# Transposes moved behind the first key block's product, a stack loaded in one piece, and four sums and three stores given to other engines

## The chip, the cores and the metric

The kernel runs on one core of a Trainium2 chip. A core has five engines with a queue of instructions each: TensorE (PE; its weight loads are shown apart as PEld), VectorE (DVE), ScalarE (ACT), GpSimd (POOL) and SyncE (SP), which here does nothing but issue DMA transfers. An engine takes its instructions in order and waits on semaphores for the others. The metric is the device time of one execution in microseconds (us); lower is better.

## The reference, cut to what matters

A block of a transformer on 2048 tokens of width 576: a modulated layer norm, attention with 32 heads of width 18 in four segments of 512 tokens with a memory carried from segment to segment, an output projection with a residual, a second modulated layer norm and a gated feed-forward network of width 4608 with a residual. All in float32.

```python
for s in range(N):                                   # N = 4 segments, L = 512
    qs, ks, vs = q[:, :, s], k[:, :, s], v[:, :, s]
    logits = jnp.einsum("bhqd,bhkd->bhqk", qs, ks) * scale + mask
    p = _softmax(logits, axis=-1)
    a_dot = jnp.einsum("bhqk,bhkd->bhqd", p, vs)
    pq = phi(qs)
    num = jnp.einsum("bhld,bhde->bhle", pq, M)
    den = jnp.einsum("bhld,bhd->bhl", pq, z)[..., None] + 1e-6
    o = g * (num / den) + (1.0 - g) * a_dot
    outs.append(o)
    pk = phi(ks)
    M = M + jnp.einsum("bhld,bhle->bhde", pk, vs)
    z = z + jnp.einsum("bhld->bhd", pk)
...
x = x + ga * (o @ wo)
h = _layernorm(x, axis=-1) * (1 + cb) + sb
x = x + gb * ((_silu(h @ w_gate) * (h @ w_up)) @ w_down)
```

## The kernel before

The program has four stages, one after the other on TensorE.

**Projections (0 to 245 us).** Queries, keys and values of all segments; queries and keys go to DRAM, split in a high and a low part so that products can run in the fast float32 format.

**Attention units (245 to 610 us).** The attention is cut into 32 units u, each of four heads of one segment (s = u // 8, q = u % 8). Four buffers hold the operands of a unit: `ks` (keys) and `qs` (queries), called a stack here; unit u uses buffer u % 4. `load_stack` (L159) fills one with four DMAs, two for each half e of its rows. In a unit two streams run side by side, written out by hand: `p2_step` (L584) forms the scores of unit u transposed (L601), their exponentials on ScalarE (L604) and a triangular cut on GpSimd (L608); `p1_step` (L173) forms the scores of unit u + 2 (L182) and their row maxima on VectorE (L187, two score banks in turn), which `mt_a` and `mt_b` transpose and `put_m` stores into two rows of that unit's stack.

A unit has 11 steps k. Each step issues a piece of both streams and then the events of the table `PAT` (L60), which has four patterns: 0 and 1 for even and odd units of the first half of a segment, 2 and 3 for even and odd units of the second half. An event is a letter; those that matter here:

- `V0` to `V3`: the products of exponentials and values for the four key blocks (`av_step`, L621). V0 and V1 belong to unit u, V2 and V3 to unit u - 1, whose sum is copied out by `E` (`ev_step`).
- `c`: four transposes of that copied output of unit u - 1 on TensorE (`comb_a`, L642) into a bank of the tag `x`, of which there are two.
- `d`: its division by the softmax sums (`comb_b`, L650 to L658 on VectorE, L659 on GpSimd).
- `M0` to `M3` and `X`: a piece of the output projection of the segment before (`wo_m`, L731) and its residual add (`wo_x`, L736), which also stores the row tile; `R`, `S`, `T`: the transposes of its input (`wo_r`, L704) and their split.
- `m`, `n`: transposing and storing the maxima of unit u + 1; `A`, `B`, `C`, `D`, `G`: the memory term.

What orders the loads is the place of their calls in this loop (L1352, L1366), since SyncE takes them in turn:

```python
load_unit(u + 3, 0)
...
for k in range(11):
    ...
    if k == 5:
        load_unit(u + 3, 1)
```

**The last output projection (610 to 636 us).** The projection of segment 3 runs by itself: eight groups of 14 matmuls (L731), four row tiles i times two halves h, in two banks in turn, so that a group needs the residual add (L736) of the group two before. Beside it VectorE and ScalarE prepare the first operands of the next stage: `y_here` (L1046 to L1050), `prep_r` (L1153, L1154), `prep_w` (L1168, L1169). `sum_o` (L1156) forms sums of the weight tiles `O`; the list `SS` names the eight places n = 8i + 4h + c of the loop where one is called. ScalarE issues the stores of the first three row tiles, SyncE that of the fourth.

**The feed-forward network (636 to 1899 us).** Products by a fast scheme with seven multiplications (L1204), then the down projection (L1308, L1325).

Of the kernel before, what the change touches and what calls it, by code (L numbers as in the profile page):

```python
# [15 lines left out]
P = 128  # L16
S = 2048
D = 576
# [39 lines left out]
E1 = 3  # L58
E2 = 2
PAT = (["", "V2", "V3 E m D", "M0", "n M1 Q G", "c", "M2 d", "V0 g", "h A0 q M3 R S X", "T Y Z B0", "A1 P V1 z B1 f C"],  # L60
# [3 lines left out]
LNA = 1  # L64
S1B, S2B, XB, WB = 2, 2, 2, 1

# [1 line left out]
def f32(ap):  # L68
    return ap.bitcast(F32)
# [3 lines left out]
def block(ctx: ExitStack, tc: tile.TileContext, x, wqk, wv, wo, beta, wgu, wd, c, w_mod, out):  # L73
    nc = tc.nc
    def pool(stk, name, bufs=1, **kw):
        return stk.enter_context(tc.tile_pool(name=name, bufs=bufs, reuse_waits="tile", **kw))
# [5 lines left out]
    def chain(*g):  # L82
        for a in g:
            yield from a

    def run(g):
        for _ in g:
            pass
# [26 lines left out]
    NB = 4  # L115
# [29 lines left out]
    xD = [dr.tile([P, 4, D], F32, tag=f"xD{s}", name=f"xD{s}") for s in range(NSEG)]  # L145
# [9 lines left out]
    NU = len(units)  # L155
    mcol, pmt, mrow = {}, {}, {}

    def load_stack(u, b, es=(0, 1)):
        s, q = units[u]  # L159
        for e in es:  # L160
            v = [d[s].rearrange("f z t -> (f z) t").rearrange("(Q a e r) t -> Q e r a t", Q=8, a=2, e=2)[q, e]
                 for d in (kD, qD)]
            r = slice(54 * e, 54 * e + 54)
            nc.sync.dma_start(f32(kst[b][r]), v[0])
            nc.sync.dma_start(f32(qst[b][r, e:4:2, :]), v[1])
# [79 lines left out]
    with ExitStack() as p1:  # L245
# [78 lines left out]
        with ExitStack() as p0:  # L324
# [41 lines left out]
            for b in range(3):  # L366
                n = P if b < 2 else 64
# [89 lines left out]
        def proj(s, t):  # L457
            hh, hl, hr = hT[s]
            pp = ps.tile([P, L], F32, tag="p", name="pp", bufs=3)
            mm14(pp, lambda k: wqkh[:, t, k, :], lambda k: wqkl[:, t, k, :], lambda k: hh[k],  # L460
                 lambda k: hl[k], lambda: hr, True)
            f = pb.tile([P, L], F32, tag="pf", name="pf")
            fh = pb.tile([P, L], F32R, tag="fh", name="fh")
            fl = pb.tile([P, L], F32R, tag="fl", name="fl")
            nc.scalar.copy(fh, pp)
            nc.scalar.copy(f, pp)
            nc.vector.tensor_tensor(fl, f, f32(fh), op=ALU.subtract)
            k0, k1 = 128 * t, min(128 * t + 128, D)
            if k0 < D:
                n = k1 - k0  # L470
                nc.sync.dma_start(kD[s][k0:k1, 0:2, :], f32(fh[:n]).unsqueeze(1).to_broadcast([n, 2, L]))
                nc.sync.dma_start(kD[s][k0:k1, 2, :], f32(fl[:n]))
            q0, q1 = max(128 * t - D, 0), 128 * t + 128 - D
            if q1 > 0:
                n = q1 - q0
                r = P - n
                nc.sync.dma_start(qD[s][q0:q1, 0:3:2, :], f32(fh[r:]).unsqueeze(1).to_broadcast([n, 2, L]))
                nc.sync.dma_start(qD[s][q0:q1, 1, :], f32(fl[r:]))
                if s > 0:
                    nc.sync.dma_start(qF[s][q0:q1, :], f[r:])  # L480
            return f
# [34 lines left out]
        for s in range(NSEG):  # L516
# [5 lines left out]
            g = chain(*gens)  # L522
# [6 lines left out]
            for t in QKORD:  # L529
# [4 lines left out]
                f = proj(s, t)  # L534
# [41 lines left out]
    opl_ = pool(p2, "op2")  # L576
    ps = pool(p2, "ps2", 2, space=PSUM)

    def load_unit(u, e):
        if u < NU:  # L580
            load_stack(u, u % NB, (e,))

    def p1_seq(u):
        if NE <= u < NU:  # L584
            for i in range(4):
                yield from p1_step(u, u % NB, 3 - i, ps, wk, 4)
# [3 lines left out]
    def p2_step(u, j):  # L590
        if u >= NU:
            return
        n = L - 128 * j
        per = L // n if n <= 256 else 1
        pt = pp_.tile([P, 4, n], F32, tag=f"P{j}", name="Pt", bufs=1)
        Pt[u, j] = pt
        for h in range(0, 4, per):
            bank = ps.tile([P, L], F32, tag="s2", name="s2", bufs=S2B)
            for g in range(h, h + per, 2):
                w = min(per, 2)  # L600
                nc.tensor.matmul(bank[:, n * (g - h):n * (g - h + w)].rearrange("p (a b) -> p a b", a=w),  # L601
                                 lhsT=kst[u % NB][0:110, g // 2, 128 * j:128 * j + 128],
                                 rhs=qst[u % NB][0:110, g:g + w, 128 * j:L], start=True, stop=True)
            nc.scalar.activation(pt[:, h:h + per, :n], bank[:, :n * per].rearrange("p (a b) -> p a b", a=per),  # L604
                                 AF.Exp, scale=SCALE)
            if h + per < 4:
                yield
        nc.gpsimd.affine_select(out=pt[:, :, :P], in_=pt[:, :, :P], pattern=[[0, 4], [1, P]], compare_op=ALU.is_ge,  # L608
                                fill=0.0, base=0, channel_multiplier=-1)
        yield  # L610
# [52 lines left out]
    def load_v(s, j):  # L663
        if j == 0:
            vq[s] = vp.tile([P, 4, VC], F32, tag="vq", name=f"vq{s}")
        nc.sync.dma_start(vq[s][:, j, :], vD[s][:, j, :])
# [5 lines left out]
    op = pool(p2r, "op", side="right")  # L672
# [37 lines left out]
    def wo_s(s, i):  # L710
        nc.scalar.copy(oT[s, i][0], pto[s, i])
# [21 lines left out]
    def wo_x(s, i, h):  # L733
        xr = oT[s, i][2]
        sl = slice(288 * h, 288 * h + 288)
        nc.vector.tensor_tensor(xr[:, sl], wps[0][:, :288], xr[:, sl], op=ALU.add)  # L736
        if h == 1 and s < 3:
            (nc.scalar if (s, i) == (2, 3) else nc.sync).dma_start(xD[s][:, i, :], xr)

    lnv = {}  # L740
# [386 lines left out]
    O, W, R, RW, DP = {}, {}, {}, {}, {}  # L1127
    later = []

    def flush():  # L1130
        while later:
            later.pop(0)()
# [20 lines left out]
        nc.scalar.copy(r[0:96, c], o[0:96, c, 2, :])  # L1153
        later.append(lambda: nc.vector.tensor_tensor(r[32:64, c], o[32:64, c, 2, :], f32(r[32:64, c]), op=ALU.subtract))  # L1154

    def sum_o(p, z, j):  # L1156
        o = O[p, z]
        d, a, b, op = ((4, 3, 2, ALU.add), (5, 4, 0, ALU.subtract), (3, 0, 3, ALU.subtract), (6, 1, 5, ALU.subtract))[j]
        nc.gpsimd.tensor_tensor(o[:, d], o[:, a], o[:, b], op=op)  # L1159

    def store_r(p, z):
        nc.scalar.dma_start(rD[p][z], f32(R[z][0:96]))
# [44 lines left out]
    T, SG, AC, AP = {}, {}, {}, {}  # L1207
# [136 lines left out]
    with tc.manual_schedule():  # L1344
# [4 lines left out]
        event("f", -1)  # L1349
        for u in range(NU + 1):  # L1350
            s, q = divmod(u, 8)
            load_unit(u + 3, 0)  # L1352
            ga = chain(*[p2_step(u, j) for j in range(4)])
            gb = p1_seq(u + 2)
            for k in range(11):
                next(ga, None)
                next(gb, None)
                if u == 17 and k == 0:
                    stage_a()
                if u == 24 and k == 0:  # L1360
                    stage_b()
                for ev in PAT[q // 4 * 2 + u % 2][k].split():
                    event(ev, u)
                for f in sched.pop(11 * u + k, ()):
                    f()
                if k == 5:  # L1366
                    load_unit(u + 3, 1)
                    if 3 <= q < 7 and s < 3:
                        load_v(s + 1, q - 3)
            run(ga)  # L1370
            run(gb)
        p2.close()
# [9 lines left out]
        xr3 = {i: load_xr(3, i) for i in range(3)}  # L1382
# [20 lines left out]
        for i in range(4):  # L1403
            for h in range(2):
                for c in range(WC):
                    n = 8 * i + 4 * h + c
                    wo_m(3, i, h, c, 2)
                    if c == 3:
                        wo_x(3, i, h)
                    flush()  # L1410
                    if i > 0 and h == 0 and c == 1:
                        nc.scalar.dma_start(xD[3][:, i - 1, :], xr3[i - 1])
                    if n in SS:
                        j = SS.index(n)
                        sum_o(0, j // 4, j % 4)
                    if n in HH:
                        y_here(HH.index(n))
                    if n in WW:
                        j = WW.index(n)
                        if j < 2:  # L1420
                            prep_r(0, 0, 0, j)
                        prep_w(0, 0, next(gw))
                if h == 1 and i < 2:
                    wo_r(3, i + 2)
                    wo_s(3, i + 2)
                    wo_t(3, i + 2)
        flush()
        nc.sync.dma_start(xD[3][:, 3, :], xr3[3])
        p2r.close()
        p5.close()  # L1430
        accp = pool(p4, "acc")
# [10 lines left out]
        n, nw = 0, PF  # L1442
# [5 lines left out]
        for t in range(2):  # L1448
            for p in range(NPR):
# [16 lines left out]
                for k in range(14):  # L1466
                    z, m = ZM[k]
# [67 lines left out]
                    if prev is not None and is_plain(*prev):  # L1535
# [3 lines left out]
                        if CH0[t][k]:  # L1539
                            f = plain(*prev, chunk)  # L1540
# [20 lines left out]
                    if is_plain(t, p):  # L1561
                        if k in DK[dl // 2]:
                            j = DK[dl // 2].index(k)
# [74 lines left out]
```

## Time and profile before

| | |
|---|---|
| time, median of 3 runs | 1902.11 us (1901.88 to 1902.49) |
| the profiled execution | 1901.1 us, of which the span from the first to the last instruction is 1899.4 us |
| granted TensorE clock, mean | 0.998 |
| busy in the span | PE 98%, PEld 82%, DVE 79%, ACT 51%, POOL 28% |
| largest groups on the chain that ended last | PE A L1204 24%, PE pd L1325 13%, PE C L1204 12%, PE pd L1308 9% |

How to read the profile's rows. A row of the timeline gives the start in us from the span's beginning, the length, engine, line of the kernel, operation, output and inputs by the program's names, the shape and a count of merged instructions; in brackets stands the idle time of the engine before it and what ended that. Matmuls are pipelined, so the distance from one start to the next is what one costs, and its length is longer. A row of the windows gives, for each engine, its busy time in that stretch. A row of the list of waits gives who waited for whom, the total, how often, and the longest.

### The profile page before, as it was taken

The numbers are of one execution on the slowest core, as the hardware profiler recorded it, in microseconds if no ns is written. First come the engines' busy times: TensorE is split into PE (matmuls) and PEld (weight loads), VectorE is DVE, ScalarE is ACT, GpSimd is POOL, SyncE is SP. The second block draws the span as 40 slices with busy tenths as digits, with TensorE's granted clock in tenths as the row PEclk, the third lists the DMA queues.
The fourth block names the chain that finished last, engine by engine and source line by source line (L and its number), as shares of the span: only waits on it lengthen the run. The fifth ranks groups of instructions, "written<-read, shape, count | busy, mean of one in ns | idle before, by whom it ended". The sixth has DMA issues, their size and how long they took to land.

```text
span 1899.4 us, 30695 instructions
## 1 busy us (share of the span) xinstructions
PE 1866.3 (98%) x10927; PEld 1559.4 (82%) x10927; DVE 1497.0 (79%) x3275; ACT 972.1 (51%) x2128; POOL 535.8 (28%) x717
## 2 busy tenths in 40 slices
PE   7999999999999899999999999999999999999999
PEld 5888856676766788888888888888888888888888
DVE  6555368878886888888888888867888888888887
ACT  4433377768766544454454454444445454454542
POOL 2000046454556544454445445400000000000000
PEclk9999999999999999999999999999999999999999
DMA  7767654546654854554554544477233332333331
GB/s 248 258 202 256 227 156 132 138 132 181 184 158 150 301 175 165 176 168 156 171 174 150 191 149 143 152 259 234 93 124 102 106 104 93 124 102 107 104 103 61
DMA packets 179424, 304.31 MB, mean 160 GB/s; under 512 B 26152, under 2 KB 107688, under 8 KB 177352
## 3 DMA queue, kind: packets, MB, share of 16 engines
q1 hardware_dynamic: 150264, 244.40, 41.4%
q10 hardware_dynamic: 29008, 57.96, 8.6%
q8 instruction: 86, 1.41, 0.3%
q14 instruction: 66, 0.54, 0.1%
HBM read 187.98 MB, written 113.77 MB: 159 GB/s over the span
## 4 chain that ended last, share of the span: by engine, by line
PE 91%; DVE 4%; DMA 2%; ACT 1%; issue 1%; SPq 1%; POOL 0%; ACTq 0%; DVEq 0%
PE A L1204 24%; PE pd L1325 13%; PE C L1204 12%; PE pd L1308 9%; PE B L1204 6%; PE pp L99 6%; PE s L601 4%; PE av L621 4%; PE s L182 3%; PE pv L99 3%; PE pw L731 2%; DMA qs<-qD 2%; PE pm L449 1%; PE pn L802 1%; DVE junk L187 1%
## 5 line engine op out<-in xcount | busy, mean ns | idle before, releaser
L1204 PE MATMUL A<-y,wh 128*128 128x512 f32 x1152 | 405.9, 393 | 1.0 <-ACT cu L1233 0.7
L187 DVE CUSTOM_DVE_ANT_0 junk<-s,tri 128x256 bf16<-128x256 f32 (+3 forms) x512 | 229.2, 487 | 74.4 <-PE s L182 67.1
L1169 DVE TENSOR_TENSOR wl<-O,wh 128x256 fp32r<-128x256 f32 x504 | 260.3, 521 | 2.8 <-ACT wh L1168 2.3
L1204 PEld LDWEIGHTS A<-y,wh 128*128 128x128 f32 x1152 | 216.6, 188 | 44.6 <-ACT cu L1233 1.1
L604 ACT ACTIVATE Pt<-s 128x512 f32<-128x512 f32 (+1 forms) x352 | 187.9, 559 | 76.2 <-PE s L601 69.7
L1204 PE MATMUL A<-y,wl 128*128 128x512 f32 x576 | 226.7, 394 | 0.0
L1159 POOL TENSOR_TENSOR O<-O 128x384 f32<-128x384 f32 x144 | 162.9, 1145 | 165.7 <-DMA O<-in_wgu_dram 71.3
L1313 DVE TENSOR_TENSOR acc<-acc,pd 128x576 f32<-128x576 f32 x216 | 162.3, 752 | 58.7 <-PE pd L1308 51.9
L1204 PE MATMUL C<-y,wh 128*128 128x512 f32 x576 | 202.6, 392 | 2.6 <-DVE cu L1227 2.6
L1168 ACT CAST wh<-O 128x256 fp32r<-128x256 f32 x504 | 196.8, 405 | 7.4 <-DVE wl L1169 3.5
L1325 PE MATMUL pd<-dh,ah 128*128 128x288 f32 x640 | 189.0, 295 | 0.0
L1325 PE MATMUL pd<-dh,al 128*128 128x288 f32 x640 | 189.0, 295 | 0.0
L1325 PE MATMUL pd<-dl,ah 128*128 128x288 f32 x640 | 188.8, 295 | 0.0
L1329 DVE TENSOR_TENSOR acc<-acc,pd 128x576 f32<-128x576 f32 x156 | 116.9, 749 | 88.8 <-PE pd L1325 88.5
L1268 ACT CAST ah<-sg 128x512 fp32r<-128x512 f32 x192 | 119.1, 620 | 82.0 <-DVE sg L1228 81.7
L601 PE MATMUL s<-qs,ks 110*128 110x512 f32 (+2 forms) x384 | 150.1, 407 | 2.1 <-ACT Pt L604 2.0
L182 PE MATMUL s<-ks,qs 108*128 108x256 f32 (+3 forms) x512 | 140.9, 327 | 6.0 <-DMA qs<-qD 3.5
L1269 DVE TENSOR_TENSOR al<-sg,ah 128x512 fp32r<-128x512 f32 x192 | 133.5, 695 | 9.1 <-ACT ah L1268 8.9
L1308 PE MATMUL pd<-dh,ah 128*128 128x288 f32 x448 | 133.0, 297 | 0.0
L1308 PE MATMUL pd<-dh,al 128*128 128x288 f32 x448 | 132.5, 296 | 0.0
L1308 PE MATMUL pd<-dl,ah 128*128 128x288 f32 x448 | 132.3, 295 | 0.0
L1204 PEld LDWEIGHTS C<-y,wh 128*128 128x128 f32 x576 | 108.3, 188 | 23.2 <-DVE cu L1227 3.0
(360 smaller groups left out, 4392.4 us busy)
## 6 DMA issues: line engine op xcount, KB each, us to landing
O<-in_wgu_dram SPq DMA_DIRECT2D x36, 768.0 KB
oD<-O ACTq DMA_DIRECT2D x36, 512.0 KB
O<-oD SPq DMA_DIRECT2D x36, 512.0 KB
ks<-kD SPq DMA_DIRECT2D x64, 216.0 KB
qs<-qD SPq DMA_DIRECT2D x64, 216.0 KB
O<-in_wgu_dram SPq DMA_DIRECT2D x36, 384.0 KB
rD<-wr ACTq DMA_DIRECT2D x36, 336.0 KB
wr<-rD SPq DMA_DIRECT2D x35, 336.0 KB
```

The lines of the kernel that those rows point to most:

```text
L99: nc.tensor.matmul(ps, lhsT=a, rhs=b, start=(k == 0), stop=(k == 13))
L182: nc.tensor.matmul(bank[:, n * (h - h0):n * (h - h0) + n], lhsT=qst[b][0:108, h, 128 * i:128 * i + 128], rhs=kst[b][0:108, h // 2, 0:n], s ...
L187: nc.vector.tensor_tensor_reduce(junk[:, :n], bank[:, n * (h - h0):n * (h - h0) + n], tri[:, L - n:], 1.0, -3e38, op0=ALU.add, op1=ALU.max ...
L601: nc.tensor.matmul(bank[:, n * (g - h):n * (g - h + w)].rearrange("p (a b) -> p a b", a=w), lhsT=kst[u % NB][0:110, g // 2, 128 * j:128 * ...
L604: nc.scalar.activation(pt[:, h:h + per, :n], bank[:, :n * per].rearrange("p (a b) -> p a b", a=per), AF.Exp, scale=SCALE)
L1159: nc.gpsimd.tensor_tensor(o[:, d], o[:, a], o[:, b], op=op)
L1168: nc.scalar.copy(wh, o)
L1169: later.append(lambda: nc.vector.tensor_tensor(wl, o, f32(wh), op=ALU.subtract))
L1204: nc.tensor.matmul(bank, lhsT=a, rhs=b, start=(first and n == 0), stop=(n == 6), skip_group_check=not first)
L1308: nc.tensor.matmul(pd[:, i, :288], lhsT=a[:, tk], rhs=w, start=(k == 0), stop=(k == 2))
L1313: nc.vector.tensor_tensor(o, o, pd[:, :, :288], op=ALU.add)
L1325: nc.tensor.matmul(pd[:, i, :288], lhsT=a[:, tk], rhs=w, start=(k == 0), stop=(k == 5))
```

## The change

```diff
-       ["V2 D", "l M0 Q", "V3 m E", "M1", "G p n A0 B0 M2", "", "M3 X A1 q c x d B1", "f", "V0 g", "", "C V1 Y h P"],
-       ["", "V2", "V3 m E", "M0", "D G M1 c n", "", "Q V0 d g R", "h", "M2 q M3 A0 S B0 X", "Z Y", "P f z V1 A1 T B1 C"],
-       ["", "V2 m", "l D n p G M0", "V3", "M1 E M2 A0", "", "M3 x c", "B0", "V0 d Q", "A1 g", "q X V1 Y B1 h P C f"])
+       ["V2 D", "l M0 Q", "V3 m E", "M1", "G p n A0 B0 M2", "", "M3 X A1 q x B1", "f", "V0 c g", "d", "C V1 Y h P"],
+       ["", "V2", "V3 m E", "M0", "D G M1 n", "", "Q V0 c R d g", "h", "M2 q M3 A0 S B0 X", "Z Y", "P f z V1 A1 T B1 C"],
+       ["", "V2 m", "l D n p G M0", "V3", "M1 E M2 A0", "", "M3 x", "B0", "V0 c Q d", "A1 g", "q X V1 Y B1 h P C f"])
...
-    def load_unit(u, e):
+    def load_unit(u):
         if u < NU:
-            load_stack(u, u % NB, (e,))
+            load_stack(u, u % NB)
...
-        if h == 1 and s < 3:
+        if h == 1:
             (nc.scalar if (s, i) == (2, 3) else nc.sync).dma_start(xD[s][:, i, :], xr)
...
-    def sum_o(p, z, j):
+    def sum_o(p, z, j, eng=nc.gpsimd):
...
-        nc.gpsimd.tensor_tensor(o[:, d], o[:, a], o[:, b], op=op)
+        eng.tensor_tensor(o[:, d], o[:, a], o[:, b], op=op)
...
-            load_unit(u + 3, 0)
+            load_unit(u + 3)
...
-                if k == 5:
-                    load_unit(u + 3, 1)
-                    if 3 <= q < 7 and s < 3:
-                        load_v(s + 1, q - 3)
+                if k == 5 and 3 <= q < 7 and s < 3:
+                    load_v(s + 1, q - 3)
...
-                    if i > 0 and h == 0 and c == 1:
-                        nc.scalar.dma_start(xD[3][:, i - 1, :], xr3[i - 1])
                     if n in SS:
                         j = SS.index(n)
-                        sum_o(0, j // 4, j % 4)
+                        sum_o(0, j // 4, j % 4, nc.vector if j > 3 else nc.gpsimd)
...
-        nc.sync.dma_start(xD[3][:, 3, :], xr3[3])
```

In patterns 1, 2 and 3 the event `c` now stands directly behind `V0`: from step 6 to step 8 in pattern 1, from 4 to 6 in pattern 2, from 6 to 8 in pattern 3. The event `d` moves from step 6 to step 9 in pattern 1; in patterns 2 and 3 it keeps its step, which is now that of `c`. Pattern 0 is as it was. All four DMAs of a stack are issued at step 0 of the unit. In the last output projection the last four of the eight sums run on VectorE, and SyncE issues all four stores, each directly behind the residual add of its row tile. Nothing that is computed changes.

More of the change, by code (lines that the diff above doesn't have):

```diff
@@ L156, in block, with load_stack @@
     mcol, pmt, mrow = {}, {}, {}
-    def load_stack(u, b, es=(0, 1)):
+    def load_stack(u, b):
         s, q = units[u]
-        for e in es:
+        for e in range(2):
             v = [d[s].rearrange("f z t -> (f z) t").rearrange("(Q a e r) t -> Q e r a t", Q=8, a=2, e=2)[q, e]
```

## The prediction

> **What bounds the kernel now.** I read the windows first, one row per stage; columns are the stretch and its length, busy us of TensorE, its weight loads, VectorE, ScalarE and GpSimd, granted clock, DMA share, GB/s.
>
> ```profile
> core 0: us, PE busy (x) PEld busy (x) DVE busy (x) ACT busy (x) POOL busy (x), PEclk, DMA share, GB/s
> 245.00:610.00 365.00, 356.21 (x2597) 238.48 (x2596) 289.03 (x1176) 270.91 (x557) 201.16 (x382) 1.00 0.53 149
> 610.00:636.00 26.00, 21.91 (x152) 21.05 (x151) 18.93 (x31) 9.54 (x21) 14.74 (x12) 0.93 0.85 317
> 636.00:1310.00 674.00, 670.25 (x3663) 588.32 (x3662) 560.54 (x860) 319.47 (x740) 294.51 (x265) 1.00 0.55 182
> ```
>
> TensorE (PE) is the bound in every stage. The diff touches two: the attention units (245 to 610 us) and the last output projection (610 to 636 us), which has 4.1 us of open idle and a clock of 0.93. What follows holds PE 670.25 of 674 us, so time won before it should arrive at the end nearly whole. Then the list of waits of the attention stage (total us, times, longest):
>
> ```profile
> PEld s L182 <- DVE mx L187: 10.3, 22, 1.3
> PE s L182 <- DMA qs<-qD: 3.5, 6, 0.9
> ```
>
> PE's waits there are short and few, for VectorE's running maxima and for the stack's query half.
>
> **The change part by part.**
>
> **Transposes behind the product.** 24 units (patterns 1, 2 and 3, eight each) issue the same four transposes (L642) later; only the neighbours change. Here is the transposes' cost alone, the product of key block 0 (L621, 512 wide) alone, and the product with other transposes (L704) directly behind it, which pattern 2 already has.
>
> ```profile
> 391.55 1.07 PE L621 MATMUL av<-Pt,vq 128*32 128x512 f32 x8
> ...
> 392.89 0.28 PE L182 MATMUL s<-ks,qs 108*128 108x256 f32 x1
> ...
> 399.75 0.60 PE L642 MATMUL px<-ident,avs 128*128 128x128 f32 x4
> ...
> 400.36 0.34 PE L182 MATMUL s<-ks,qs 108*128 108x384 f32 x1
> 400.54 0.34 PE L601 MATMUL s<-qs,ks 110*128 110x384 f32 x1
> ...
> 400.98 1.07 PE L621 MATMUL av<-Pt,vq 128*32 128x512 f32 x8
> 401.98 0.66 PE L704 MATMUL pto<-ident,o 128*128 128x128 f32 x4
> ...
> 402.65 0.34 PE L182 MATMUL s<-ks,qs 108*128 108x384 f32 x1
> ```
>
> From start to start, less the one score matmul in between (0.18 for 384 columns, 400.36 to 400.54; 0.24 for 512, in the next fence): product alone 1.34 - 0.24 = 1.10, transposes alone 0.61 - 0.18 = 0.43, both together 1.67 - 0.18 = 1.49. Together they cost 0.04 to 0.06 less than 1.53. Units 19, 25 and 27 and six of pattern 2 have transposes behind that product already, so 15 of 24 gain: 15 x 0.05 = 0.8 us. Bounds: 0.6 (15 x 0.04) to 1.2 (24 x 0.05).
>
> **The stack at step 0.** SyncE issues the second half's two DMAs (ks, qs) right behind the first half's, not behind the two stores of step 4. The number of DMAs is the same.
>
> ```profile
> 429.92 0.29 SPq L164 DMA_DIRECT2D ks<-kD  x1
> ...
> 437.56 0.49 SPq L164 DMA_DIRECT2D ks<-kD  x1
> ...
> 442.24 0.40 PE L182 MATMUL s<-ks,qs 108*128 108x512 f32 x1
> 442.48 0.40 PE L601 MATMUL s<-qs,ks 110*128 110x512 f32 x1
> 443.17 0.47 PE L182 MATMUL s<-ks,qs 108*128 108x512 f32 x1 [0.29 <-DMA qs<-qD]
> ...
> 265.91 0.47 PE L182 MATMUL s<-ks,qs 108*128 108x512 f32 x1 [0.92 <-DMA qs<-qD]
> ...
> 467.27 0.47 PE L182 MATMUL s<-ks,qs 108*128 108x512 f32 x1 [0.74 <-DVE mx L187]
> ```
>
> The first half goes out at 429.92, the second at 437.56; the second then moves some 7 us forward, against a longest wait of 0.9. The six waits (3.5 us) go. A seventh, 467.27, stands under VectorE, whose maximum was long done; it has the same place in its unit (the second score, the first to read the second half), so I count it as DMA: 4.2 us. Behind the loads in SyncE's queue stand the two small copies of the maxima into the same stack, due a unit later. SyncE pays 0.3 to 0.5 us per issue twice, in a queue that waits anyway. DMA share is 0.53, so the burst is covered; with that cover gone those copies would be late, at up to the 0.9 us of a late qs.
>
> **What is late next: VectorE in pattern 1.** There the combine (L650 to L658, 0.87 us: 438.11 to 438.98) moves from step 6 to step 9, into the unit's end:
>
> ```profile
> 438.11 0.25 DVE L650 RECIPROCAL r<-px 128x16 f32<-128x16 f32 x1
> ...
> 438.98 0.55 DVE L187 CUSTOM_DVE_ANT_0 junk<-s,tri 128x384 bf16<-128x384 f32 x1
> ...
> 440.59 0.42 DVE L187 CUSTOM_DVE_ANT_0 junk<-s,tri 128x256 bf16<-128x256 f32 x1 [0.37 <-PE s L182]
> ...
> 441.29 0.29 DVE L187 CUSTOM_DVE_ANT_0 junk<-s,tri 128x128 bf16<-128x128 f32 x1
> ...
> 442.13 0.08 DVE L187 DVE_READ_ACCUMULATOR2_ANT mx<- 128x1 f32 x1
> ```
>
> Step 10's four maxima, now 441.29 to 442.13, would end near 443.05. Their score bank is the one that the next unit's second score needs; without the DMA it would start 0.24 behind 442.48, at 442.72, so it waits some 0.35. That is a new wait in 8 units. Ends: nothing (VectorE's idle takes it) and the whole 0.87, 0 to 7.0 us. I take 0.3 each, near the worked case, 2.4 us. Queued behind the combine are those maxima and, on GpSimd, the add and the L192 chain for the next unit's transpose of the maxima, which TensorE reaches two steps later. Stack and combine together: 4.2 - 2.4 = 1.8 us won (bounds -2.8 to +4.2).
>
> **In patterns 2 and 3** the combine now waits on VectorE for a product before its transposes. I cost it at nothing, since that is when VectorE starves:
>
> ```profile
> 400.74 0.56 DVE L187 CUSTOM_DVE_ANT_0 junk<-s,tri 128x384 bf16<-128x384 f32 x1 [0.49 <-PE s L182]
> ...
> 403.02 0.56 DVE L187 CUSTOM_DVE_ANT_0 junk<-s,tri 128x384 bf16<-128x384 f32 x1 [0.37 <-PE s L182]
> ```
>
> PE gives no score for the microsecond of the product, and the combine's 0.87 ends about when the next score comes. The uncovered price is in the slower rival.
>
> **Four sums on VectorE, three stores on SyncE.**
>
> ```profile
> 616.73 10.37 POOL L1159 TENSOR_TENSOR O<-O 128x384 f32<-128x384 f32 x8
> ...
> 622.55 1.11 DVE L1169 TENSOR_TENSOR wl<-O,wh 128x256 fp32r<-128x256 f32 x1
> ...
> 624.07 1.01 DVE L1154 TENSOR_TENSOR wr<-O,wr 32x512 fp32r<-32x512 f32 x1
> 625.11 1.13 DVE L1169 TENSOR_TENSOR wl<-O,wh 128x256 fp32r<-128x256 f32 x1
> 626.16 1.48 DVE L1048 TENSOR_TENSOR y<-yh,y 128x512 fp32r<-128x512 f32 x1
> ...
> 627.93 0.41 DVE L1169 TENSOR_TENSOR wl<-O,wh 128x256 fp32r<-128x256 f32 x1
> ...
> 628.86 0.68 DVE L1048 TENSOR_TENSOR y<-yh,y 128x512 fp32r<-128x512 f32 x1
> ...
> 624.18 0.37 PE L731 MATMUL pw<-woh,oh 128*128 128x288 f32 x1 [1.56 <-DVE xr L736]
> ...
> 628.06 0.40 PE L731 MATMUL pw<-woh,oh 128*128 128x288 f32 x1 [1.79 <-DVE xr L736]
> ...
> 626.10:629.50 3.40, 1.60 (x13) 1.44 (x11) 3.40 (x7) 0.93 (x2) 0.99 (x1) 1.00 1.04 349
> 629.50:632.90 3.40, 3.40 (x17) 3.40 (x16) 1.88 (x5) 1.06 (x3) 0.00 (x0) 0.50 0.55 217
> ```
>
> GpSimd sums from 616.73 to 627.10. While it does, VectorE's operations between two SBUF tiles take 1.1 to 1.5 us; once it stops, the same lines take 0.41 and 0.68. PE waits twice for the delayed residual add (3.35 us), and the clock is then 0.50 for 3.4 us, which costs 1.7. With half the sums gone GpSimd ends near 622, and four operations shrink from 4.73 to 2.18 (0.41 + 0.68 + 0.41 + 0.68). The first wait falls to 1.56 - 0.70 = 0.86; the second nearly goes, since its add comes 2.55 earlier (0.1 left); the next group waits some 0.4 for its add. So 3.35 - 1.36 = 2.0, and the clock has no window as idle as 626.1 to 629.5 (PE 1.60 of 3.40): 1.7 more. Sum 3.7 us. The moved sums cost VectorE 4 x 0.55 (between 0.41 for 256 and 0.68 for 512), but they stand behind the add that frees the last projection group, where only later weights wait. The stores leave ScalarE's queue for SyncE's, where what stands behind them waits for the last store as before; were that cover gone, a load would be three issues late (3 x 0.4). Bounds of this part: 0 (VectorE, with the sums, sets the pace) to 5.05 (both waits and the clock).
>
> The Trainium skill (SBUF — State Buffer, "Who interferes with whom") calls the port pair of VectorE and GpSimd an exclusive lock. The rows agree: 1.48 against 0.68. From that, Perfetto Trace Analysis, "Optimizing Scalar/DVE Operations", warns that moving work between these two might not help; this would make the part 0 and the sum 2.6. TensorE: Matmul & The Clock Gate, Part 1, has the clock fall after an idle window of about 3.4 us; no window here was idle throughout (PE 1.60), so the trace disagrees, and by the page the 1.7 would not be these waits' doing.
>
> **Sum.** 0.8 + 1.8 + 3.7 = 6.3 us. The profiled execution took 1901.1 us with a span of 1899.4; it would take 1894.8. Runs had a median of 1902.1, 1.0 above it: 1895.8 us.
>
> **The rivals.**
> - VectorE's lateness eats the DMA gain: if the whole 0.87 is paid in all eight units, stack and combine give 4.2 - 7.0 = -2.8 and the sum is 1.7: 1900.4. For: 289 of 365 us busy. Against: the 0.37 idle ahead of 440.59. Chance 0.15.
> - The sums on VectorE take what the lock gave back (the skill's warning): 2.6, 1899.5. For: VectorE is busy 18.93 of 26. Against: PE waits for adds that stand ahead of the moved sums. Chance 0.10.
> - Slower: in patterns 2 and 3 VectorE blocks at the combine through the product (1.07), the two score banks fill and PE stands. It decides where VectorE's lag at step 9 exceeds the half microsecond it idles at that place. If half of it shows in 16 units, 8.6, and pattern 1 pays 7.0: 15.6 - 8.7 (0.8 + 4.2 + 3.7) = 6.9 slower, 1909. Chance 0.08.
> - More is won: pattern 1 pays nothing and both projection waits go: 0.8 + 4.2 + 5.0 = 10.0, 1892.1. Chance 0.10.
>
> **How the numbers follow.** The forecast has the remaining 0.57, with its own range of 1893.5 to 1898. A measurement tells 0.2%, 3.8 us, from no change. Faster by more than that: nearly all of the forecast, the last rival, and the milder half of the first two, 0.74. Within: 0.18. Slower: 0.08. The range 1892 to 1900 leaves out the slower rival and the edges.
>
> **What would show it.** Waits of L182 for qs gone from the list; L182's wait for mx grown, at the second score of units behind pattern 1; L642 behind L621; in the projection no clock of 0.5, VectorE's L1169 and L1048 at 0.41 and 0.68 after 622, and the first L1204 about 6 us earlier in the span. I am wrong if L182's waits for mx grow by over 5 us, or the projection still takes 26 us.

## The result: slower, 1910.33 us

The changed kernel took 1910.33 us (median of 5 runs, 1908.49 to 1913.24) beside 1902.11 us (1901.07 to 1903.88) for the kernel before on the same chip: a ratio of 1.0040, with a 95% interval of 1.0026 to 1.0054. The prediction, 1895.8 us and faster, was wrong in sign. The profiled execution of the changed kernel had a span of 1908.6 us, 9.2 us more than the 1899.4 of before.

First the windows, with the stretches cut at the same events in both kernels: the start of the first and of the last L601 (attention), of the first L1204, and of the 169th matmul into `A`. Columns as in the prediction. The kernel before:

```profile
0.00:244.90 244.90, 232.31 (x1346) 197.67 (x1346) 129.01 (x301) 99.21 (x182) 25.44 (x58) 0.99 0.71 237
244.90:607.02 362.12, 353.71 (x2570) 237.44 (x2568) 289.03 (x1176) 269.36 (x554) 199.35 (x380) 1.00 0.53 148
607.02:635.27 28.25, 23.78 (x178) 21.59 (x177) 18.40 (x29) 11.09 (x23) 16.55 (x15) 0.94 0.89 322
635.27:731.50 96.23, 92.69 (x482) 79.25 (x480) 83.09 (x134) 46.90 (x107) 50.18 (x46) 1.00 0.60 207
731.50:1899.40 1167.90, 1163.78 (x6362) 1023.42 (x6360) 977.42 (x1637) 545.51 (x1262) 244.33 (x219) 1.00 0.44 140
```

The changed kernel:

```profile
0.00:247.34 247.34, 234.70 (x1345) 198.92 (x1346) 128.59 (x301) 99.31 (x182) 25.35 (x58) 0.99 0.71 235
247.34:616.48 369.14, 357.09 (x2569) 236.78 (x2568) 287.32 (x1173) 269.51 (x554) 199.47 (x379) 1.00 0.50 145
616.48:641.68 25.20, 22.31 (x177) 20.10 (x176) 18.34 (x37) 10.91 (x23) 11.82 (x11) 1.00 0.96 340
641.68:739.82 98.14, 93.20 (x481) 79.13 (x480) 84.29 (x136) 47.25 (x107) 50.42 (x46) 1.00 0.61 207
739.82:1908.60 1168.78, 1164.44 (x6362) 1023.73 (x6360) 979.56 (x1637) 546.58 (x1262) 244.38 (x219) 1.00 0.43 140
```

Row by row, after less before: +2.44, +7.02, -3.05, +1.91, +0.88, together +9.20. The loss is in attention. The last projection is 3.05 shorter, and the first products behind it are 1.91 longer; whether the second follows from the first is looked at below. The first row has no edit in it; over all the profiled executions below the first L601 started between 243.8 and 247.8 us, so its 2.44 is no effect of the change.

Now the lists of waits of the attention stage (total us, times, longest). Three rows of the kernel before that the prediction did not show:

```profile
PE s L182 <- DVE mx L187: 1.9, 4, 0.7
PE s L601 <- ACT Pt L604: 2.0, 7, 0.6
PE av L621 <- POOL Pt L608: 0.7, 2, 0.4
```

The changed kernel:

```profile
PEld s L182 <- DVE mx L187: 12.8, 33, 1.1
...
PE s L182 <- DVE mx L187: 4.1, 9, 0.7
PE s L601 <- ACT Pt L604: 4.1, 13, 0.7
...
PE av L621 <- POOL Pt L608: 1.9, 2, 1.2
...
PE s L601 <- DMA qs<-mr: 1.4, 1, 1.4
```

The waits of L182 for `qs` (3.5 us, six) are gone, as predicted. Three kinds have grown: for VectorE's maxima (4.1 from 1.9, and 12.8 on the weight loads, where the prediction's row had 10.3), for ScalarE's exponentials (4.1 from 2.0) and for GpSimd's cut (1.9 from 0.7). One is new, for the stored maxima. Which edit made which is what the experiments take apart. Since the units are the same work in every kernel, the sharpest reading is unit by unit: the distance from one unit's first L601 to the next one's.

### The profile page after: what moved, and what is told of

Read it like the earlier page. It is cut to its first block, busy times and chain, and to the rows that moved or that the text cites. A ratio compares the mean times of both kernels' runs of the same rounds, so it can differ in the third digit from the quotient of the medians.

```text
span 1908.6 us, 30690 instructions
## 1 busy us (share of the span) xinstructions
PE 1871.7 (98%) x10927; PEld 1558.7 (82%) x10927; DVE 1498.1 (78%) x3279; ACT 973.6 (51%) x2128; POOL 531.5 (28%) x713
## 4 chain that ended last, share of the span: by engine, by line
PE 91%; DVE 3%; ACT 2%; DMA 1%; POOL 1%; issue 1%; SPq 0%; DVEq 0%; ACTq 0%; POOLq 0%
PE A L1204 23%; PE pd L1325 13%; PE C L1204 12%; PE pd L1308 9%; PE B L1204 6%; PE pp L99 6%; PE s L601 4%; PE av L621 4%; PE s L182 4%; PE pv L99 3%; PE pw L731 3%; PE px L642 1%; PE pn L802 1%; PE pm L449 1%; ACT Pt L604 1%; DVE junk L187 1%
## 5 line engine op out<-in xcount | busy, mean ns | idle before, releaser
L1204 PE MATMUL A<-y,wh 128*128 128x512 f32 x1152 | 406.2, 393 | 3.2 <-ACT tc L1233 2.0
L1204 PEld LDWEIGHTS A<-y,wh 128*128 128x128 f32 x1152 | 216.6, 188 | 48.0 <-ACT tc L1233 2.5
L1204 PE MATMUL A<-y,wl 128*128 128x512 f32 x576 | 226.7, 394 | 0.0
L1204 PE MATMUL C<-y,wh 128*128 128x512 f32 x576 | 202.6, 392 | 1.8 <-DVE cu L1227 1.8
L601 PE MATMUL s<-qs,ks 110*128 110x512 f32 (+2 forms) x384 | 149.5, 405 | 5.9 <-ACT Pt L604 4.1
L182 PE MATMUL s<-ks,qs 108*128 108x256 f32 (+3 forms) x512 | 142.0, 329 | 4.4 <-DVE mx L187 4.4
L1204 PEld LDWEIGHTS C<-y,wh 128*128 128x128 f32 x576 | 108.3, 188 | 22.3 <-DVE cu L1227 2.2
```

The costliest lines, as they stand in the source:

```text
L182: nc.tensor.matmul(bank[:, n * (h - h0):n * (h - h0) + n], lhsT=qst[b][0:108, h, 128 * i:128 * i + 128], rhs=kst[b][0:108, h // 2, 0:n], s ...
L1204: nc.tensor.matmul(bank, lhsT=a, rhs=b, start=(first and n == 0), stop=(n == 6), skip_group_check=not first)
```

## The experiments

Lengths are those of the five stretches above; a unit's length is as just said. Times are medians, with the kernel before run on the same chip (1903.2 to 1903.4 us in these three sets).

| run | time, us | ratio to before | attention | projection | first products |
|---|---|---|---|---|---|
| before | | | 362.1 | 28.3 | 96.2 |
| the change | 1910.33 | 1.0040 (1.0026 to 1.0054) | 369.1 | 25.2 | 98.1 |
| e1_projection | 1902.83 | 0.9997 (0.9986 to 1.0009) | 364.9 | 24.3 | 97.8 |
| e2_stack | 1898.37 | 0.9974 (0.9963 to 0.9985) | 357.2 | 26.8 | 97.2 |
| e3_table | 1912.63 | 1.0047 (1.0032 to 1.0063) | 369.9 | 27.7 | 98.6 |
| e4_no_table | 1896.15 | 0.9958 (0.9941 to 0.9974) | 357.3 | 24.3 | 99.2 |
| f1_pat1 | 1902.13 | 0.9996 (0.9987 to 1.0005) | 362.8 | 24.2 | 98.5 |
| f2_pat23 | 1903.23 | 1.0000 (0.9991 to 1.0009) | 362.2 | 25.2 | 99.1 |
| f3_pat1_d8 | 1896.11 | 0.9961 (0.9949 to 0.9974) | 357.6 | 24.3 | 98.6 |
| f4_pat2_d7 | 1912.05 | 1.0046 (1.0033 to 1.0058) | 371.9 | 25.2 | 98.9 |
| f5_late3 | 1896.32 | 0.9960 (0.9946 to 0.9974) | 357.2 | 24.3 | 98.1 |
| f6_sums | 1895.06 | 0.9955 (0.9942 to 0.9969) | 356.8 | 24.3 | 97.2 |
| f7_stores | 1898.52 | 0.9972 (0.9962 to 0.9981) | 356.0 | 26.8 | 97.9 |

In e4_no_table, f1_pat1, f2_pat23 and f4_pat2_d7 the first products hold 3.4 us at a clock of 0.50.

### The parts one by one

**The last projection alone** (e1_projection): the kernel before with these lines of the change.

```diff
-                        sum_o(0, j // 4, j % 4)
+                        sum_o(0, j // 4, j % 4, nc.vector if j > 3 else nc.gpsimd)
...
-        if h == 1 and s < 3:
+        if h == 1:
```

> The kernel before with only the edits of the last output projection (four sums on VectorE, the stores on SyncE). Theory (the table of steps carries the loss): this part is won as the changed kernel's trace shows it, the projection 3.0 us shorter (610 to 636 us stage: 28.0 to 25 us from the last score to the first L1204), of which up to 1.7 may be lost again in the first products of the feed-forward network; whole time 1.3 to 3.5 us below before. Rival (the four sums only move VectorE's work into the feed-forward network): the stretch up to 670 us is as long as before and the time is within 1 us of before.

Measured: no difference that the runs can tell, where 1.3 to 3.5 us had been expected. The profiled execution had the projection 3.95 us shorter (28.25 to 24.30), the products behind it 1.6 longer, and unit 18, which no edit touches, 2.76 longer. About half of that is two waits for the halves of the stack (0.82 and 0.59, where the kernel before had none and 0.29), the rest a clock of 0.50 for 3.4 us right behind them, from 447.95.

**The stack alone** (e2_stack).

```diff
-            load_unit(u + 3, 0)
+            load_unit(u + 3)
...
-                if k == 5:
-                    load_unit(u + 3, 1)
-                    if 3 <= q < 7 and s < 3:
+                if k == 5 and 3 <= q < 7 and s < 3:
```

> The kernel before with only the stack loaded in one piece at step 0. Theory: the seven waits of L182 for qs (4.2 us) go, the copies of the maxima are late once, in unit 3 (1.4 us), and the attention units are 2 to 4 us shorter. Rival (the burst is what made the changed kernel slower): L601 waits for qs<-mr in several units and the attention units are as long as before or longer by up to 5 us.

Measured: 0.26% faster, attention 4.9 us shorter.

**The table alone** (e3_table): the three rows of `PAT`, and nothing else.

> The kernel before with only the new table of steps. Theory: the transposes had covered TensorE's waits for ScalarE's exponentials, and the combine of pattern 1 is late for the next unit's second score: attention units 4 to 7 us longer than before (unit 30 alone 2 us), time 4 to 7 us above before. Rival (the stack load carries the loss): the attention units are within 1 us of before.

Measured: 0.47% slower, attention 7.8 us longer.

**All but the table** (e4_no_table): the changed kernel with the old `PAT`.

> The changed kernel with the table of before: stack in one piece, sums on VectorE, stores on SyncE. Theory: 3 to 7 us below before (2 to 4 from the stack, 1.3 to 3.5 from the projection). Rival (the stack load carries the loss): above before. If the first 30 us are 2.4 us longer here too, with no edit there, that part of the changed kernel's profile belongs to the execution and not to the change.

Measured: 0.42% faster than before, and attention back at 357.3. What follows from the four: the loss is the table's. It costs 7.8 us alone and 11.8 (369.1 less 357.3) where the stack comes early, so with the new table the stack is worth 0.8 (369.9 less 369.1) and not 4.9. The units show part of why: with the old table the early stack shortens units 2, 10, 12 and 18 by 0.45 to 1.12 each, with the new one by 0.10 at most. There the old wait for `qs` and the new one for VectorE hold up the same second score, and only the longer one counts. Most of the rest is units 21 and 29, which the table alone had already made 1.02 and 0.39 shorter.

### The table taken apart

**Pattern 1 alone** (f1_pat1), on e4_no_table:

```diff
-       ["V2 D", "l M0 Q", "V3 m E", "M1", "G p n A0 B0 M2", "", "M3 X A1 q c x d B1", "f", "V0 g", "", "C V1 Y h P"],
+       ["V2 D", "l M0 Q", "V3 m E", "M1", "G p n A0 B0 M2", "", "M3 X A1 q x B1", "f", "V0 c g", "d", "C V1 Y h P"],
```

> The run without any of the new table took 1896.15 us with 357.3 us from the first to the last L601 of attention; the whole change 1910.33 and 369.1. Here pattern 1's row alone is moved. Theory (VectorE gets to the unit's last maxima too late, because the combine now stands right ahead of them at step 9): the second score of the units behind pattern 1 (2, 4, 10, 12, 18, 20, 26, 28) waits 0.2 to 0.7 us for DVE mx L187 where it waited for nothing, these units are 0.6 to 1.1 us longer each, attention takes about 364 (357.3 + 7) and the run about 1903. Rival (the cost lies in patterns 2 and 3, where the transposes no longer fill TensorE's wait for a score bank): attention stays within 1.5 of 357.3 and the run at 1896 to 1898.

**Pattern 1 with the combine left in the step of its transposes** (f3_pat1_d8): one letter away from the run before.

```diff
-"V0 c g", "d", "C V1 Y h P"
+"V0 c d g", "", "C V1 Y h P"
```

> As the run with pattern 1's row alone, but the combine stays in the step of its transposes (step 8) and not one step later. If the loss in pattern 1 comes from the combine's place one step later, just ahead of the last maxima, half of that run's loss or more is gone: attention about 360, the run about 1899. If it comes from the transposes' place (the combine can't start before the product and the transposes are done, wherever it is issued) attention stays within 1 of that run's, about 363 to 364. A third outcome, longer than that run by over 1: VectorE blocks at the combine while scores wait behind it.

Measured: pattern 1 alone took attention from 357.3 to 362.8 and the run to 1902.13, near the theory. With `d` one step earlier nearly all of it was gone, not half: 357.6 and 1896.11. So the transposes' new place in pattern 1 costs 0.3 us; the combine's place costs 5.2. VectorE's timeline at the end of unit 17 shows how. With `d` in step 9:

```profile
441.22 0.42 DVE L187 CUSTOM_DVE_ANT_0 junk<-s,tri 128x256 bf16<-128x256 f32 x1 [1.19 <-PE s L182]
...
441.92 0.25 DVE L650 RECIPROCAL r<-px 128x16 f32<-128x16 f32 x1
442.21 0.62 DVE L651 TENSOR_TENSOR r<-r,omg 128x16 f32<-128x16 f32 x1
...
443.24 0.28 DVE L187 CUSTOM_DVE_ANT_0 junk<-s,tri 128x128 bf16<-128x128 f32 x1
...
444.07 0.08 DVE L187 DVE_READ_ACCUMULATOR2_ANT mx<- 128x1 f32 x1
```

With `d` in step 8, the same unit (this execution runs about 3.1 us earlier here):

```profile
437.62 0.26 DVE L650 RECIPROCAL r<-px 128x16 f32<-128x16 f32 x1 [0.71 <-PE px L642]
437.91 0.17 DVE L651 TENSOR_TENSOR r<-r,omg 128x16 f32<-128x16 f32 x1
...
438.50 0.42 DVE L187 CUSTOM_DVE_ANT_0 junk<-s,tri 128x256 bf16<-128x256 f32 x1
```

While TensorE works on the product, VectorE has nothing to do. In step 8 the combine falls into that hole: VectorE idles 0.71 until the transposes are there, and the combine is done by 438.5, soon after the next scores have come. In step 9 VectorE idles through the whole hole (1.19); the combine's input is ready before the hole ends, but the combine is queued behind two maxima. It then does it at the busiest place, just ahead of the last four maxima. And there it takes 1.32 us (441.92 to 443.24) in place of 0.88, since L651 takes 0.62 and not 0.17 beside GpSimd's cut, which this row of GpSimd's timeline in the same run shows:

```profile
442.17 0.64 POOL L608 TENSOR_SCALAR_AFFINE_SELECT Pt<-Pt 128x512 f32<-128x512 f32 x1 [2.03 <-ACT Pt L604]
```

The Trainium skill (SBUF — State Buffer, "Who interferes with whom") says that a VectorE operation with two inputs in SBUF contends with a GpSimd operation that reads SBUF; L651 has both its inputs there, and the trace agrees. Unit 17 is the worst case: L651 took 0.34 to 0.62 in units 1, 3, 9, 11 and 17, and 0.17 or 0.18 in 19, 25 and 27. The units behind those three still grew by 0.53 to 0.68, so most of the loss is the place and not the slower L651. What it costs TensorE, in the run with `d` in step 9:

```profile
442.54 0.50 PE L601 MATMUL s<-qs,ks 110*128 110x512 f32 x1
...
444.21 0.50 PE L182 MATMUL s<-ks,qs 108*128 108x512 f32 x1 [0.70 <-DVE mx L187]
444.65 0.42 PE L621 MATMUL av<-Pt,vq 128*32 128x256 f32 x4
```

and in the run with `d` in step 8:

```profile
439.40 0.50 PE L601 MATMUL s<-qs,ks 110*128 110x512 f32 x1
...
440.22 0.44 PE L182 MATMUL s<-ks,qs 108*128 108x512 f32 x1
440.59 0.64 PE L621 MATMUL av<-Pt,vq 128*32 128x256 f32 x8
```

The second score waits for a score bank that VectorE still reads. The bracket says 0.70; over the same matmuls in both runs, from the first of these starts to the last it is 2.11 against 1.19, so the wait's price is 0.92. A matmul's row is longer than its share of the pipeline, and the idle time that a list of waits gives is the smaller number. The seven units 2, 10, 12, 18, 20, 26 and 28 grew by 0.53 to 0.99 each over e4_no_table, 5.4 together; unit 4, expected among them, did not. Pattern 1's own units 9, 11 and 17 became 0.06 shorter.

**Patterns 2 and 3 alone** (f2_pat23), on e4_no_table: the last two rows of `PAT` from the change.

> Patterns 2 and 3 alone are moved. Theory: units 5, 6, 7, 22, 28 and 31 lose 0.2 to 0.5 us each, since L601 then waits for ACT Pt L604 where the transposes stood, and unit 30 about 2, where L659's add stands ahead of L608 on GpSimd: attention 357.3 + 4.4 = about 362, the run about 1900.5. Rival (all the loss is VectorE's in pattern 1): attention within 1 of 357.3, the run within 1 of 1896.

Measured: attention 362.2, as the theory had it, and the run 1903.23, higher than the 1900.5 expected; 0.9 of that is lost in the projection, as shown below. Eight units grew by 0.31 to 0.59 (4, 5, 6, 7, 20, 22, 28 and 31) and unit 30 by 2.04; unit 3, outside these patterns, happened to be 1.05 shorter (the next section says what varies there). Unit 4 in TensorE's timeline, first e4_no_table with the transposes (L642) at their old place:

```profile
289.77 0.34 PE L182 MATMUL s<-ks,qs 108*128 108x384 f32 x1
289.95 0.60 PE L642 MATMUL px<-ident,avs 128*128 128x128 f32 x4
...
291.40 1.07 PE L621 MATMUL av<-Pt,vq 128*32 128x512 f32 x8
```

then f2_pat23 with them behind the product:

```profile
290.00 0.34 PE L182 MATMUL s<-ks,qs 108*128 108x384 f32 x1
290.50 0.45 PE L601 MATMUL s<-qs,ks 110*128 110x384 f32 x1 [0.16 <-ACT Pt L604]
...
291.62 1.06 PE L621 MATMUL av<-Pt,vq 128*32 128x512 f32 x8
292.62 0.66 PE L642 MATMUL px<-ident,avs 128*128 128x128 f32 x4
293.03 0.42 PE L601 MATMUL s<-qs,ks 110*128 110x384 f32 x1
```

From the L182 to the product it is 1.63 us with the transposes in between and 1.62 without them. They had filled the time in which the next score waits for ScalarE to read its bank; taken away, they leave that wait (0.16 of it in a bracket). Behind the product nothing waits, and there they cost 0.41 in full (292.62 to 293.03). So the transposes were nearly free where they stood. In the other units that grew they cost 0.41 to 0.49 behind the product too, and by the start of the product their leaving had won 0.09 at most.

Unit 30 has another reason. GpSimd in f2_pat23:

```profile
598.62 1.04 POOL L659 TENSOR_TENSOR o<-o,tmp 128x288 f32<-128x288 f32 x1 [1.43 <-DVE tmp L658]
...
600.30 0.82 POOL L608 TENSOR_SCALAR_AFFINE_SELECT Pt<-Pt 128x512 f32<-128x512 f32 x1
```

and TensorE there:

```profile
601.18 0.85 PE L621 MATMUL av<-Pt,vq 128*32 128x384 f32 x8 [1.15 <-POOL Pt L608]
...
611.73 1.01 PE L621 MATMUL av<-Pt,vq 128*32 128x256 f32 x16 [1.26 <-POOL Pt L608]
```

The combine's add L659 stands ahead of the cut L608 in GpSimd's order; it waits for the later combine, and V1 waits for the cut. From start to start that wait costs 1.22 of unit 30's 2.04; a wait of the same kind at the unit's first product costs 0.39 more, and the transposes 0.43. The last row shows the wait a third time, behind the last L601: 1.26, where e4_no_table has 0.38. That is why the projection takes 24.2 to 24.3 us with the sums moved and the old patterns 2 and 3, and 25.2 with the new ones. Pattern 1's 5.5 and these 5.9 (4.8 and unit 3's 1.05) make 11.4 of the 11.8 that the table cost in attention.

**The combine one step later in pattern 2** (f4_pat2_d7), the whole change with:

```diff
-"Q V0 c R d g", "h"
+"Q V0 c R g", "h d"
```

> The whole change, with one thing more: in pattern 2 the combine goes one step later (step 7), behind GpSimd's L608 of key block 1. Theory (unit 30 loses 2 us because the add L659, which waits for the later combine, stands ahead of that L608 on GpSimd, and V1 waits for L608): V1's wait of 1.15 for POOL Pt L608 in unit 30 is gone and the unit is 1 to 2 us shorter than in the whole change; the other units of pattern 2 within 0.5; attention about 367.5 to 368, the run 1908 to 1909. Rival (L608 itself is slower or its input late): V1 waits for L608 as before, unit 30 within 0.3 of the whole change's.

Measured: GpSimd now does the cut first, and unit 30 is 1.23 us shorter than in the change (0.83 over e4_no_table in place of 2.06).

```profile
609.40 0.64 POOL L608 TENSOR_SCALAR_AFFINE_SELECT Pt<-Pt 128x512 f32<-128x512 f32 x1 [0.71 <-ACT Pt L604]
610.00 0.80 POOL L659 TENSOR_TENSOR o<-o,tmp 128x288 f32<-128x288 f32 x1
```

That part of the theory holds. But the expected 1908 to 1909 was missed: the run took 1912.05, since pattern 2's other units paid for the later combine. Units 12, 14, 20 and 22 grew by a further 0.54 to 0.75 over the change. There a product of the memory term (L802) writes to a bank of the tag `x`, and it now waits for the combine to leave one. In unit 12:

```profile
386.65 0.98 PE L802 MATMUL pn<-mbd,pq 128*128 128x76 f32 x6 [0.31 <-DVE tmp L658]
```

The change has no such wait, this run four (1.2 us in all). In units 4 and 6 it is L182 that waits, as in f1_pat1, and its waits for `mx` went from 4.1 us in 9 to 5.5 in 13. A combine a step behind its transposes costs more than it frees here too.

### The stack in units 3 and 4

The stack alone shortened eight units by 0.45 to 1.20 each (6.4 together) and lengthened unit 3 by 1.50. SyncE's queue in e2_stack there:

```profile
276.24 0.36 SPq L906 DMA_DIRECT2D woraw<-in_wo_dram  x1
...
278.29 0.34 SPq L165 DMA_DIRECT2D qs<-qD  x1
280.78 1.15 SPq L170 DMA_DIRECT2D qs<-mr  x2
```

and the next unit's first score:

```profile
287.30 0.47 PE L601 MATMUL s<-qs,ks 110*128 110x512 f32 x1 [1.44 <-DMA qs<-mr]
```

The copies of the maxima (L170) now go out behind both halves, with two other loads ahead. **The second half late in unit 3 alone** (f5_late3), on e4_no_table:

```diff
-            load_unit(u + 3, 1)
+            if u != 3:
+                load_unit(u + 3, 1)
...
                 if k == 5:
+                    if u == 3:
+                        load_unit(u + 3, 1)
```

> The old table, the whole stack at step 0, the sums and the stores (1896.15 us), but in unit 3 alone the second half is loaded at step 5 as before. Theory (that unit's 1.2 to 1.6 us wait of L601 for qs<-mr comes from the copies of the maxima queueing behind the second half's transfers): the wait is gone, unit 3 is about 1.5 us shorter, attention takes about 355.9 and the run about 1894.6. Rival (the copies are late for another reason, the row they copy being late): L601 waits over 1 us there as before, attention stays at 357.3.

Measured: the wait is gone and unit 3 as in the kernel before, so the copies did queue behind the second half. But the time stayed: attention 357.2, the run 1896.32. Unit 4 is 1.5 longer again, because its second score now waits for that half:

```profile
285.50 0.47 PE L182 MATMUL s<-ks,qs 108*128 108x512 f32 x1 [1.23 <-DVE mx L187]
```

(The row blames VectorE; with the half loaded at step 0 the wait isn't there, so it is the DMA, as the prediction argued for 467.27.) In this unit two transfers are due at one time, and in these runs the order only set which of them was late. How late varies between executions: the wait for `qs<-mr` was 1.2 to 1.6 in six and 0.5 in three. The Trainium skill (DMA: Bandwidth & Descriptors, "Queues, rings and completion order") has one issuer's descriptors taken in the order of its ring; these runs agree, though sharing of the bandwidth would look the same here.

### The last projection

**Sums without the stores** (f6_sums) and **stores without the sums** (f7_stores), both with the old table and the whole stack at step 0.

> Old table, whole stack at step 0, the four sums on VectorE, but the three stores stay on ScalarE. Last L601 to first L1204 took 24.30 with sums and stores and 26.82 without both; the 97 us of products behind it 99.16 and 97.15. Theory (the sums alone make the projection shorter and they make the first products later): 24.3 and 99.2, the run 1896. Rival (the stores' move shares in either): the projection over 25, or the products behind it under 98.

> Old table, whole stack at step 0, the three stores on SyncE, but all eight sums stay on GpSimd. Theory (the stores cost and gain nothing): projection 26.8, the products behind it 97.2, the run 1898.4 as with the stack alone. Rival (a store in SyncE's queue holds a load up, or ScalarE gains from their absence): one of the two stretches is over 0.7 away from these.

The windows of the projection and of the products behind it, f6_sums:

```profile
601.73:626.01 24.28, 22.31 (x177) 20.10 (x176) 17.17 (x33) 11.10 (x23) 11.64 (x11) 1.00 1.00 361
626.01:723.19 97.18, 93.19 (x482) 79.04 (x480) 84.30 (x136) 47.16 (x107) 51.19 (x46) 1.00 0.61 208
```

and f7_stores, with one of the two emptiest windows of 3.4 us in its projection and the window behind it (the last section says where such windows lie):

```profile
601.74:628.57 26.83, 22.35 (x177) 20.11 (x176) 18.41 (x29) 10.88 (x23) 16.56 (x15) 1.00 0.97 338
628.57:726.48 97.91, 93.36 (x481) 79.17 (x480) 83.85 (x134) 47.22 (x107) 50.40 (x46) 1.00 0.60 203
618.67:622.08 3.41, 2.08 (x14) 1.88 (x14) 3.35 (x4) 2.90 (x7) 3.15 (x3) 1.00 1.05 362
622.08:625.50 3.42, 2.71 (x19) 2.64 (x20) 3.39 (x8) 0.00 (x0) 0.00 (x0) 1.00 0.98 329
```

and the products of e3_table, which has neither the sums nor the stores moved:

```profile
642.97:741.57 98.60, 93.66 (x482) 78.92 (x481) 84.75 (x134) 46.91 (x107) 51.27 (x46) 1.00 0.60 203
```

The sums make the projection 2.5 us shorter (26.83 to 24.28), and the products behind it are not longer for it: 97.18, as in e2_stack (97.15). The 99.2 expected there came from e4_no_table, whose products have a clock of 0.50 for 3.4 us in them, from 656.4. With the stores alone the products took 97.91 and with both 98.05 in f5_late3, but this does not show that the stores cost anything: e3_table, without them, took 98.60 with the clock at 1.00, and f7_stores took 0.9972 of the time of the kernel before, e2_stack 0.9974. For the same reason the 1.91 us that the change seemed to lose in these products is not shown to come from the edits; the 96.23 of the kernel before is the shortest of the thirteen profiled executions.

The 3.05 us of the projection are thus three things: 2.5 won by the sums; 1.4 from the kernel before, whose profiled execution had a clock of 0.50 there that e2_stack, with the same projection, has not (28.25 and 26.82); and 0.9 lost by the table. f7_stores, e2_stack and e3_table have both old waits for the residual add, and their clock stays at 1.00.

## Why the prediction was wrong, by its steps

- **Transposes behind the product, 0.8 us won.** This step came out with the wrong sign. It priced the transposes at 0.43 in one place and 0.39 in the other, both read off rows, but never asked what TensorE would do in the place they left. In patterns 2 and 3 it waited there (1.63 and 1.62 us). The rows of busy time were right; the saving holds only where TensorE had other work to move up, as in units 9, 11 and 17 (0.06 each). Measured in f2_pat23: attention 5.9 us longer without unit 3's 1.05, of which 1.6 is unit 30's waits for GpSimd, so some 4.3 lost by the transposes where 0.8 had been won.
- **Pattern 1's combine, 2.4 lost.** Right in kind, queue and place, too small: 5.2 us, inside its bounds of 0 to 7.0. Two terms were off. A wait was priced by an estimated start at 0.35 and then taken at 0.3, where seven units paid 0.53 to 0.99; and in five of eight units L651 was slowed beside GpSimd, so that the combine took up to 1.32, not 0.87. The predicted hole in VectorE's work was real, but pattern 1's combine had been put behind it.
- **The combine in patterns 2 and 3, nothing.** Right for VectorE: L182's waits for `mx` are 1.1 us in three both with and without these rows. But the step left out GpSimd, where the combine's add then held up the cut: 1.6 us in unit 30 and 0.9 in the projection. The slower rival came out near in time, 1909, but by luck: in 2 and 3 VectorE did not hold TensorE up.
- **The stack, 4.2 won.** Right by itself: 4.9 in attention, and the wait at 467.27 was the DMA's. The named cover, that the burst hides behind a DMA share of 0.53, failed once, in unit 3, for up to 1.6. What the step missed is that its gain and the combine's loss fall on the same waits: with the new table the stack was worth 0.8.
- **Sums and stores, 3.7 won.** The waits' part, estimated at 2.0, measured 2.5. The clock's 1.7 cannot be counted as won: of the four profiled executions with both waits only the kernel before has the dip, and of the nine with them shortened none. Whether the waits made it, which the prediction's sentence on the Trainium skill (TensorE: Matmul & The Clock Gate, Part 1) doubted, stays open. That the stores cost or won anything is not shown.
- **What follows is full, so time arrives nearly whole.** For the sums it did within the spread of the times: of the 2.5 us, 0.4 arrived in e1_projection, 2.2 between e2_stack and e4_no_table and 3.5 between f7_stores and f6_sums. The longer first products of the change are not shown to be the edits' doing.
- **The signs.** Neither of the two signs of being wrong that the prediction named appeared: L182's waits for `mx` grew by 4.7 us (10.3 and 1.9 to 12.8 and 4.1), not over 5, and the projection took 25.2. Neither looked at TensorE's own work behind the product, where most of the transposes' loss lies and no wait shows it.

## What to carry to other kernels

Before moving work to a place where it is cheaper, read what its engine would wait for in the place it leaves: work that fills a wait is free, and packing it elsewhere makes it paid (here 0.41 us and more each time). When a consumer moves with its producer, put it in the consumer engine's hole, ahead of what is queued there, not one step behind: here one letter in a table was worth 5.2 us. Follow it on through every engine: its add on GpSimd stood ahead of a cut that TensorE needed. Price a wait from start to start of the instructions around it, and count two waits on the same instruction once.

## What the runs showed of the hardware that was not expected

- L651, a multiplication of 16 columns with both inputs in SBUF, took 0.17 or 0.18 us with GpSimd idle and up to 0.97 when it started inside an operation of GpSimd. In f1_pat1 it was slower in ten units, and in each it ended 0.03 us behind the GpSimd operation: it waited for the whole of it. In two units a cut started at the same time as L651 and went on for longer, and there L651 took 0.18.
- Half-clock stretches come and go in executions of kernels that do not differ there: one at 447.95 us within attention in e1_projection, one at 656.4 in e4_no_table, and the projection's of the kernel before (629.5) was absent in e2_stack, e3_table and f7_stores. In each execution the changes of the clock lie whole multiples of 3.413 us apart (kernel before: 25.35, 28.76, 629.51 and 632.92; 604.16 is 177 of them), so they fall on a grid, whose place differs between executions. On it the same wait can fill one window or lie across two: ahead of the dip of the kernel before a window had 1.60 us of TensorE's work, while the emptiest in f7_stores' projection had 2.08. How empty a window is by these rows doesn't decide it alone: after 1.60 (f3_pat1_d8, 646.93) and 1.76 (e2_stack, 621.74) the clock stayed at 1.00, after 2.00 (e1_projection, 444.54) it fell. The Trainium skill (TensorE: Matmul & The Clock Gate, Part 1) has the clock judged by a window that runs freely, whatever the kernel does; the grid agrees.
- Of the versions run, the old table with the whole stack at step 0 and the four sums on VectorE is the best, 1895.06 us, 0.45% below the kernel before; the others with the old table and the stack at step 0 and sums lie within their spread of it.
